# Padding tiles that move the operands of the matmuls within 512 bytes

## The chip, the cores and the metric

One core of one Trainium2 chip runs the kernel. The metric is the device time of one execution in microseconds; 892.1 us is the median of three executions of the kernel before (891.85 to 892.5).

## What is computed

Attention over q, k, v of shape 8 x 8 x 576 x 64 (batch, heads, tokens, head dimension), then a two-layer product over all 4608 tokens. Attention is the sum of two parts: a coarse one over tokens averaged in fours, and a local one in which a token sees three neighbours on either side.

```python
out_d = sm_attn(q_d, k_d, v_d)              # over 144 averaged tokens
out_up = np.repeat(out_d, 4, axis=2)
out_local = ...                             # softmax over |i - j| < 4
x = (out_up + out_local)                    # -> 4608 x 512
h = x @ w_in                                # 512 -> 2048
g = np.maximum(0.01 * h, h)
out = g @ w_out                             # 2048 -> 512
```

## The kernel before

The tokens are cut into ten chunks (0 to 9). Of each chunk the attention part leaves x, transposed, in a tile of the tag x0 or x1 (they alternate): a high half and a low half in fp32r, since every fp32 product is made of three fp32r matmuls (high by high, high by low, low by high). The weights are kept on the chip as high and low halves, too: `wi0` to `wi15` for the first layer, `woh`, `wol` for the second, 128 of the 2048 inner features per index f.

PE then runs two products, chunk by chunk and f by f:

- `up_proj`, L1118: hp += w_in[f] by x. The stationary operand is 128 columns of `wi`, the moving operand is 256 (chunks 0 and 1), 384 (chunks 2 and 3) or 512 columns of x. Twelve matmuls make one bank `hp`.
- `leaky`, L1139 to L1142: ACT writes gh, the high half of the leaky result, and the full result; DVE writes gl, what is left. Both have 512 columns, in three buffers each.
- `down_proj`, L1164: acc += g by w_out[f]. Here the stationary operand is 128 columns of gh or gl, the moving one is 512 columns of `woh` or `wol`: for each 128 tokens the triple (woh, gh), (wol, gh), (woh, gl).

Chunks 8 and 9 go through `up_proj` together at the end, in a scheme with seven products in place of eight (`finale`, L1419). Its stationary operands are `wi` and the sums `sh`, `sl` of weights (made by POOL and ACT in `combine_1`); its moving operands are x of chunk 8, `bh`, `bl`, and four sums T1 to T4 with a high half in a buffer of x1 and low halves in `lo`, `r00`, `r01`, `r10`. These sums come from the last local results: POOL makes them (L944, L1020), DVE reduces them, they go through a buffer in DRAM, DVE adds (L1239), ACT copies the high halves (L1285) into the x1 buffer that chunk 7 has left, and DVE subtracts (L1239 again). Each PE group of three matmuls loads its weights anew, one load to a matmul.

POOL and DVE make the local part: POOL multiplies (L944 for scores, L1020 for values), DVE reduces. All this runs beside the products and feeds the next chunks. The order of the work on each engine is worked out when the kernel is built, by a planner (`Order`) that takes each step's cost and due rank; it knows sizes and engines and no addresses. Each engine runs its instructions in that order.

A tile lies at a byte offset that is the same in all partitions. Pools on the left side are stacked from below (`const`, then `wk`, then those that follow one another above it: `su`, `late`, `last`, `fin1`), each tag of a pool in the order in which it was first asked for; pools on the right side end at the top of the memory. The `wk` pool holds, in this order, olot, x1, x0, three gh, three gl. Nearly all tiles are multiples of 512 bytes, so the byte offsets of the matmuls' operands are these, taken modulo 512 (a slice of a tile keeps it, as slices step by 512 or 2048 bytes):

| tile | pool | offset | modulo 512 |
| --- | --- | --- | --- |
| wi0 to wi8, wol, woh for f = 0 to 8 | const | 896 to 74623 | 384 |
| x1, x0 | wk | 78720, 95104 | 384 |
| gh, gl (three each) | wk | 111488 to 123775 | 384 |
| wi9 to wi15, wol, woh for f = 9 to 15 | late, last | 123776 to 181119 | 384 |
| r11, r10, r00, r01, bh, bl, sr, sh, sl | fin1 | 181120 to 217983 | 384 |
| lo, then sp | fin2, right side | 221152, 225248 | 480, 480 |
| zero operands of the first bf16 matmuls (L342): moving, stationary | x1 | 14592 and 14336 bytes into x1 | 256 bytes apart |
| transposes of the first batch (L606): identity, probabilities | const, su | | 96 to 352 bytes apart |

Of the kernel before, what the change touches and what calls it, by code (L numbers as in the profile page):

```python
# [7 lines left out]
F32 = mybir.dt.float32  # L8
F32R = mybir.dt.float32r
# [80 lines left out]
OMAX = max(c[1] for c in CHUNKS[1:])  # L90
# [142 lines left out]
def attn_moe(ctx: ExitStack, tc, qkt, vm, vr, vmb, vrb, qb, kb, vb, vwb, band, identb, w_in, w_out, ident, edge, out):  # L233
# [3 lines left out]
    wk = ctx.enter_context(tc.tile_pool(name="wk", bufs=1))  # L237
# [11 lines left out]
    def slot(*tags):  # L249
        return (yield ("slot", tags, 0))  # L250

    def sb(s, shape, dtype, pool=None):
        tag = s.tag
        pool = pool or (wk if tag in KEPT else atp if tag in LAND else axp)
        return pool.tile(shape, dtype, name=tag, tag=tag, bufs=bufs[tag])

    def bank(s):
        return ps.tile([128, 512], F32, name=s.tag, tag=s.tag, bufs=bufs[s.tag])

    def op(eng, n, *after, times=1, lock=False):  # L260
        if eng == "PE":
            dur = n
        else:
            a, k = COST[eng]
            dur = times * a + k * n
        return (yield ("op", eng, dur, max((0.0,) + after), 0, after, lock))
# [9 lines left out]
    def wait(name, n=1):  # L276
        return (yield ("wait", name, n))
# [31 lines left out]
    def weight(f, k):  # L309
        f0, _, wis, *ts = max((w for w in wts if w[0] <= f), key=lambda w: w[0])  # L310
        return [w[:, f - f0] for w in ts] if k else [wis[f - f0][:, j] for j in range(2)]
# [5 lines left out]
    weight_tiles(const, 0, FSPLIT)  # L317
    w_out_v = w_out.rearrange("(f p) e -> f p e", p=128)

    stage = [wk.tile([128, bufs["stage"] + 1, HALFS * DM], U16, name="x1", tag="x1", bufs=bufs["x1"])]  # L320
    heads = [stage[0][:, bufs["stage"], i * 2 * DM:(i + 1) * 2 * DM].bitcast(I32) for i in range(bufs["head"])]
    for h in heads:
# [773 lines left out]
    def up_proj():  # L1096
        i = 0
        while i < len(STEPS):
            ch, a, z, f = STEPS[i]
            n = z - a  # L1100
            per = 0.0135 + n / 2400
            m = 2 if (ch, a, f) == (0, 0, 0) else 1
            if f == 0:
                tx = 0.0 if m > 1 else (yield from wait(("x", ch, a), LANDED[ch, a]))
            hps = []
            for k in range(m):
                tw = yield from wait(("w", f + k, 0))
                s_h = yield from slot("hp")
                hps.append((s_h, bank(s_h), weight(f + k, 0), tw))
            xh, xl = (x[:, :, a:z] for x in xt[ch])  # L1110
            for c in range(NC):
                if m > 1:
                    tx = yield from wait(("x", 0, 0, c))
                ws = slice(c * 128, (c + 1) * 128)
                for k, (s_h, hp, w, tw) in enumerate(hps):
                    t = yield from op("PE", 3 * per, tx, tw, s_h.t)
                    for j, (h, x) in enumerate(((1, xh), (1, xl), (0, xh))):
                        nc.tensor.matmul(hp[:, :n], w[h][:, ws], x[:, c], start=c + j == 0, stop=c == NC - 1 and j == 2)  # L1118
                    if c == NC - 1:
                        od.spawn(-205.082, leaky(i + k, n, s_h, hp, t))  # L1120
            if f == NF - 1:
                od.signal(("done", ch), t)
            i += m
# [3 lines left out]
    def leaky(i, n, s_h, hp, t):  # L1127
        pair, second = HALF.get(i, (None, 0))
        if second:
            yield from wait(("pair", pair))  # L1130
            s_g, s_l, gh, gl = pairs.pop(pair)
        else:
            s_g, s_l = (yield from slot("gh")), (yield from slot("gl"))
            gh, gl = sb(s_g, [128, OMAX], F32R), sb(s_l, [128, OMAX], F32R)
            if i in HALF:
                pairs[pair] = s_g, s_l, gh[:, n:], gl[:, n:]
                od.signal(("pair", pair))
        t = yield from op("ACT", 2 * n, t, s_g.t, times=2)
        nc.scalar.activation(out=gh[:, :n], in_=hp[:, :n], func=AF.Prelu, alpha=0.01)  # L1139
        nc.scalar.activation(out=hp[:, :n], in_=hp[:, :n], func=AF.Prelu, alpha=0.01)  # L1140
        t = yield from op("DVE", n, t, s_l.t)
        nc.vector.tensor_tensor(out=gl[:, :n], in0=hp[:, :n], in1=gh[:, :n].bitcast(F32), op=ALU.subtract)  # L1142
        s_h.free(t)
        gs[i] = s_g, s_l, gh, gl
        od.signal(("g", i), t)
# [73 lines left out]
    def unit(pool, tag, shape, dtype):  # L1219
        return fin[pool].tile(shape, dtype, name=tag, tag=tag, bufs=1)  # L1220
# [105 lines left out]
    def follow(key, p, held):  # L1326
# [7 lines left out]
        def first():  # L1334
            t = yield from get("P1")
            s_1, s1 = yield from place()
            t = yield from snap(key, "s1", A(), s1, t, s_1.t)
            t2 = yield from get("P2")
            t = yield from added(B(), s1, ALU.add, t, t2)
            s_1.free(t)  # L1340
            od.spawn(-44.395, leaky(("g", 2 * p), EN, *held["B"], t))

        def rest():
            t = yield from get("P6")
            s_2, u2 = yield from place()
            t2 = yield from snap(key, "u2", A(), u2, t, s_2.t)
            t = yield from get("P7")
            s_3, u3 = yield from place()
            t3 = yield from snap(key, "u3", A(), u3, t, s_3.t)
            t4 = yield from get("P4")  # L1350
            t = yield from added(D(), u3, ALU.add, t3, t4)
            od.spawn(-28.453, leaky(("g", 2 * p + 1), EN, *held["D"], t))
            t4 = yield from get("P3")
            t2 = yield from added(C(), u2, ALU.add, t2, t4)
            s_2.free(t2)
            t3 = yield from added(C(), u3, ALU.subtract, t3, t2)
            s_3.free(t3)
            tg, G = yield from stored(p)
            t = yield from get("P5")
            t = yield from snap(key, "c22", A(), G[:, 1], t, tg)  # L1360
            held["A"][0].free(t)
            t3 = yield from added(C(), G[:, 1], ALU.add, t, t3)
            t = yield from op("ACT", EN, t3)
            nc.scalar.activation(out=G[:, 0], in_=C(), func=AF.Prelu, alpha=0.01)
            held["C"][0].free(t)
            od.signal(("kept", 2 * p), t)
            t = yield from op("ACT", EN, t)
            nc.scalar.activation(out=G[:, 1], in_=G[:, 1], func=AF.Prelu, alpha=0.01)
            od.signal(("kept", 2 * p + 1), t)
# [24 lines left out]
    def finale():  # L1394
        yield from wait(("over", LAST - 2))
        yield from wait("cleared2")
        fin["sp"] = unit(2, "sp", [128, bufs["sp"], EN], F32)
        per = 3 * (0.0135 + EN / 2400)
        for p in range(NP):
            key, held = ("pair", p), {}  # L1400
            ws = [weight(2 * p + i, 0) for i in range(2)]
            raws = dict(A11=[w[:, :256] for w in ws[0]], A12=[w[:, 256:] for w in ws[0]], A22=[w[:, 256:] for w in ws[1]])
            follow(key, p, held)
            for name in ORDER:
                b, a, x = PRODUCTS[name]
                if b not in held:
                    s_b = yield from slot("hp", "pt")
                    held[b] = s_b, bank(s_b)
                tb = held[b][0].t
                if name in BEFORE:  # L1410
                    tb = max(tb, (yield from wait((key, BEFORE[name]))))
                ta = (yield from wait(("sw", 0, p))) if a[0] == "S" else 0.0
                tx = yield from wait(x)
                w = SW[0, p][a] if a[0] == "S" else raws[a]
                for c in range(2):
                    t = yield from op("PE", per, tb, ta, tx)
                    for j, (h, m) in enumerate(((1, 1), (1, 0), (0, 1))):
                        acc = held[b][1][:, :EN]
                        nc.tensor.matmul(acc, w[h][:, c * 128:(c + 1) * 128], T[x][m][:, c],  # L1419
                                         start=c + j == 0 and name not in BEFORE, stop=c == 1 and j == 2, skip_group_check=True)  # L1420
                od.signal((key, name), t)
            od.signal(("paired", p), t)
        od.signal(("done", LAST - 1), t)
# [162 lines left out]
```

## Time and profile before

| | |
| --- | --- |
| median of 3 executions | 892.1 us (891.85 to 892.5) |
| the profiled execution, its time | 893.24 us |
| its span, first to last instruction | 891.5 us |
| matmuls in the trace | 4815, one weight load each |
| mean granted clock of PE | 0.993 of full speed |

The profile shows one execution. PE are the matmuls, PEld the weight loads that run beside them, DVE, ACT and POOL the other engines. A matmul's recorded duration is longer than the distance to the next one's start, as matmuls overlap: 512 columns are recorded with some 390 ns. In the chain that ended last, each piece is counted only up to where the next one begins, so a piece of 24 matmuls divided by 24 is that distance. The granted clock is 1.00 at 2.4 GHz and 0.50 at 1.2 GHz.

### The profile page before, as it was taken

How to read it: one execution, taken by the hardware profiler on the slowest of the kernel's cores; microseconds unless marked ns; L12 is line 12 of the kernel's file. 1: busy time of each engine (PE TensorE's matmuls, PEld its weight loads, DVE VectorE, ACT ScalarE, POOL GpSimd, SP SyncE). 2: the span in 40 equal slices, each digit the busy share in tenths (PEclk: the TensorE clock that was granted, in tenths of full speed). 3: DMA queues.
4: the chain of work that ended last, by engine and by line, in shares of the span. 5: the costliest groups of instructions: out<-in, count | busy, mean ns of one | idle time of the engine just before them, and what ended most of it. 6: DMA issues, size and time to landing. Idle time of an engine off the chain costs nothing.

```text
span 891.5 us, 13603 instructions
## 1 busy us (share of the span) xinstructions
PE 872.8 (98%) x4815; PEld 721.1 (81%) x4815; DVE 639.4 (72%) x952; ACT 461.4 (52%) x1288; POOL 628.9 (71%) x316
## 2 busy tenths in 40 slices
PE   6999999999999999999999999999999999999998
PEld 3687878988899888887888888778878888888886
DVE  5888989888896988898788977887786443323322
ACT  3898866656463744466345635623443244435421
POOL 3434478798999899999998899889976433374000
PEclk9999999999999999999999999999999999999999
DMA  9878764555453563455455535534344000000001
GB/s 336 278 234 293 241 187 133 191 167 186 140 154 111 180 189 113 139 160 171 119 148 174 171 107 160 158 100 116 115 113 137 3 24 24 1 1 1 24 24 48
DMA packets 67684, 119.67 MB, mean 134 GB/s; under 512 B 8608, under 2 KB 34720, under 8 KB 67616
## 3 DMA queue, kind: packets, MB, share of 16 engines
q1 hardware_dynamic: 67616, 118.80, 42.9%
q8 instruction: 38, 0.62, 0.3%
q14 instruction: 30, 0.25, 0.1%
HBM read 106.19 MB, written 12.58 MB: 133 GB/s over the span
## 4 chain that ended last, share of the span: by engine, by line
PE 86%; DVE 6%; DMA 4%; ACT 3%; issue 1%; SPq 0%; POOL 0%; DVEq 0%; POOLq 0%; ACTq 0%
PE acc L1164 35%; PE hp L1118 32%; PE hp L1419 4%; PE pt L1419 4%; DMA qk<-in_qkt_dram 3%; PE hp L1164 2%; PE pt L1164 2%; PE pt L688 1%; DVE xloc L1026 1%; PE pt L707 1%; PE pt L751 1%; DMA stage<-in_w_out_dram 1%; PE pt L710 1%; ACT x L374 1%; DVE gl L1142 0%
## 5 line engine op out<-in xcount | busy, mean ns | idle before, releaser
L1118 PE MATMUL hp<-x,wi 128*128 128x512 f32 (+2 forms) x1632 | 333.7, 356 | 4.1 <-DVE gl L1142 4.1
L1118 PEld LDWEIGHTS hp<-x,wi 128*128 128x128 f32 x1632 | 277.2, 189 | 45.6 <-DVE gl L1142 7.5
L1020 POOL TENSOR_TENSOR prod<-v,sx 128x1344 f32<-128x1344 f32 x84 | 264.3, 3148 | 29.3 <-DVE xloc L1026 16.8
L944 POOL TENSOR_TENSOR prod<-q,k 128x1344 f32<-128x1344 f32 x84 | 261.5, 3114 | 27.4 <-DVE wi L389 8.8
L1164 PE MATMUL acc<-woh,gh 128*128 128x512 f32 x512 | 202.4, 395 | 0.0
L1164 PE MATMUL acc<-wol,gh 128*128 128x512 f32 x512 | 199.9, 390 | 0.0
L1164 PE MATMUL acc<-woh,gl 128*128 128x512 f32 x512 | 199.8, 390 | 0.0
L1139 ACT ACTIVATE gh<-hp 128x512 fp32r<-128x512 f32 (+2 forms) x140 | 73.6, 526 | 143.5 <-PE acc L1164 130.2
L1026 DVE TENSOR_REDUCE xloc<-prod 128x192 f32<-128x1344 f32 x84 | 129.7, 1546 | 14.9 <-POOL prod L1020 14.5
L950 DVE TENSOR_REDUCE s<-prod 128x21 f32<-128x1344 f32 x84 | 129.2, 1538 | 9.7 <-POOL prod L944 9.3
L1142 DVE TENSOR_TENSOR gl<-hp,gh 128x512 fp32r<-128x512 f32 (+2 forms) x140 | 82.8, 594 | 58.5 <-ACT hp L1140 56.2
L1164 PEld LDWEIGHTS acc<-woh,gh 128*128 128x128 f32 x512 | 96.2, 188 | 20.6 <-issue 2.4
L1164 PEld LDWEIGHTS acc<-woh,gl 128*128 128x128 f32 x512 | 96.1, 188 | 20.7 <-DVE gl L1142 0.2
L1164 PEld LDWEIGHTS acc<-wol,gh 128*128 128x128 f32 x512 | 96.2, 188 | 18.0
L1140 ACT ACTIVATE hp<-hp 128x512 f32<-128x512 f32 (+2 forms) x140 | 72.9, 520 | 0.0
L1239 POOL TENSOR_TENSOR sl<-sr,sh 128x1024 fp32r<-128x1024 f32 x8 | 19.2, 2399 | 73.4 <-ACT sh L1243 73.4
L989 ACT COPY sx<-s 32x84 f32<-32x84 f32 x168 | 43.8, 261 | 11.9 <-POOL s L980 9.9
L1323 DVE TENSOR_TENSOR pt<-pt,sp 128x512 f32<-128x512 f32 x12 | 8.4, 699 | 56.4 <-PE pt L1419 31.0
L1050 DVE TENSOR_TENSOR pt<-pt,outd 128x128 f32<-128x128 f32 x126 | 40.1, 322 | 3.1
L445 DVE TENSOR_REDUCE v_d<-vs 128x128 f32<-128x512 f32 (+1 forms) x53 | 35.5, 670 | 5.6 <-DMA vs<-in_vrb_dram 4.4
L1239 DVE TENSOR_TENSOR gl<-wi,gh 128x512 fp32r<-128x512 f32 x14 | 9.7, 692 | 28.3 <-ACT gh L1243 28.3
L742 ACT ACTIVATE pd<-pd,st_d 112x144 f32<-112x144 f32 x72 | 24.5, 405 | 8.9 <-DVE st_d L739 8.8
(228 smaller groups left out, 1127.5 us busy)
## 6 DMA issues: line engine op xcount, KB each, us to landing
k<-in_kb_dram SPq DMA_DIRECT2D x84, 288.0 KB, 3.3
qk<-in_qkt_dram SPq DMA_DIRECT2D x32, 576.0 KB, 4.3
v<-in_vb_dram SPq DMA_DIRECT2D x84, 192.0 KB, 2.6
q<-in_qb_dram SPq DMA_DIRECT2D x84, 96.0 KB, 2.3
vs<-in_vmb_dram SPq DMA_DIRECT2D x28, 256.0 KB, 3.3
out_dram<-olot SPq DMA_DIRECT2D x28, 256.0 KB, 2.1
vs<-in_vrb_dram SPq DMA_DIRECT2D x28, 192.0 KB, 2.7
x<-in_w_out_dram SPq DMA_DIRECT2D x9, 511.8 KB, 6.4
```

The costliest lines, as they stand in the source:

```text
L944: behind(nc.gpsimd.tensor_tensor(out=prv, in0=q[:, :nj].unsqueeze(2).to_broadcast([128, nj, W, D]), in1=view(k, 0, [[D, nj], [D, W], [1, D]]),
L950: nc.vector.tensor_reduce(out=s[:, u, p, :nj], in_=prv, axis=AX.X, op=ALU.add)
L989: nc.scalar.copy(out=both[32 * g:32 * g + 32, :, h], in_=sv[src:src + 32])
L1020: behind(nc.gpsimd.tensor_tensor(out=prv, in0=view(v, 0, [[1, nj], [nv, ROWS], [1, W]]), in1=s[:, p].unsqueeze(2).to_broadcast([128, nj, R ...
L1026: nc.vector.tensor_reduce(out=xl_t[:, :nj, p], in_=prv, axis=AX.X, op=ALU.add)
L1050: nc.vector.tensor_tensor(out=part, in0=part, in1=view(outd[b], 2 * u * SD + o, [[2 * COLS // FAC, ROWS], [sm, cm], [sr, cr]]), op=ALU.add)
L1118: nc.tensor.matmul(hp[:, :n], w[h][:, ws], x[:, c], start=c + j == 0, stop=c == NC - 1 and j == 2)
L1139: nc.scalar.activation(out=gh[:, :n], in_=hp[:, :n], func=AF.Prelu, alpha=0.01)
L1140: nc.scalar.activation(out=hp[:, :n], in_=hp[:, :n], func=AF.Prelu, alpha=0.01)
L1142: nc.vector.tensor_tensor(out=gl[:, :n], in0=hp[:, :n], in1=gh[:, :n].bitcast(F32), op=ALU.subtract)
L1164: nc.tensor.matmul(acc, g[:, ts], w[h], start=f + j == 0, stop=f == NF - 1 and j == 2)
L1419: nc.tensor.matmul(acc, w[h][:, c * 128:(c + 1) * 128], T[x][m][:, c], start=c + j == 0 and name not in BEFORE, stop=c == 1 and j == 2, sk ...
```

## The change

Three tiles are added that no instruction reads or writes: 128 bytes per partition in the pool `wk` ahead of x1, 128 bytes in `wk` between gh and gl (in `leaky`, at the first step alone), and 96 bytes in the pool `fin2` (`unit` asks a pool for a tile).

```diff
     w_out_v = w_out.rearrange("(f p) e -> f p e", p=128)
 
+    wk.tile([128, 32], F32, name="shift0")
     stage = [wk.tile([128, bufs["stage"] + 1, HALFS * DM], U16, name="x1", tag="x1", bufs=bufs["x1"])]
...
             s_g, s_l = (yield from slot("gh")), (yield from slot("gl"))
-            gh, gl = sb(s_g, [128, OMAX], F32R), sb(s_l, [128, OMAX], F32R)
+            gh = sb(s_g, [128, OMAX], F32R)
+            if not i:
+                wk.tile([128, 32], F32, name="shift1")
+            gl = sb(s_l, [128, OMAX], F32R)
             if i in HALF:
...
         yield from wait("cleared2")
+        unit(2, "shift2", [128, 24], F32)
         fin["sp"] = unit(2, "sp", [128, bufs["sp"], EN], F32)
```

## Rows read from the trace of the kernel before

**Rows 1.** The page, part 1: busy time, share of the span, instructions of each engine.
```profile
PE 872.8 (98%) x4815; PEld 721.1 (81%) x4815; DVE 639.4 (72%) x952; ACT 461.4 (52%) x1288; POOL 628.9 (71%) x316
```
**Rows 2.** The page, part 4: the chain that ended last, by engine and by line.
```profile
PE 86%; DVE 6%; DMA 4%; ACT 3%; issue 1%; SPq 0%; POOL 0%; DVEq 0%; POOLq 0%; ACTq 0%
PE acc L1164 35%; PE hp L1118 32%; PE hp L1419 4%; PE pt L1419 4%; DMA qk<-in_qkt_dram 3%; PE hp L1164 2%; PE pt L1164 2%; PE pt L688 1%; DVE xloc L1026 1%; PE pt L707 1%; PE pt L751 1%; DMA stage<-in_w_out_dram 1%; PE pt L710 1%; ACT x L374 1%; DVE gl L1142 0%
```
**Rows 3.** The chain in order of time: start us, us, what; 256, 384, 512 columns.
```profile
171.58 2.87 PE hp L1118 x24
...
225.85 4.18 PE hp L1118 x24
...
427.65 5.44 PE acc L1164 x24
433.09 5.44 PE hp L1118 x24
```
**Rows 4.** PE in order of time near 6 us, and a stretch's busy times and clock.
```profile
5.74 0.81 PE L342 MATMUL acc<-x 128*128 128x512 bf16 x3
...
6.17 0.38 PE L342 MATMUL acc<-x 128*128 128x512 bf16 x1
...
6.00:6.50 0.50, 0.50 (x3) 0.06 (x1) 0.00 (x0) 0.00 (x0) 0.00 (x0) 1.00 0.89 249
```
**Rows 5.** PE in order of time near 21 us, the fp32 transposes.
```profile
20.45 0.27 PE L606 MATMUL pt<-id_sb,v 128*128 128x128 f32 x1
...
20.77 0.49 PE L606 MATMUL pt<-id_sb,v 128*16 128x128 f32 x3
```
**Rows 6.** PE near 209 us, and busy times of PE, PEld, DVE, ACT, POOL, then PEclk.
```profile
208.97 0.84 PE L1118 MATMUL hp<-x,wi 128*128 128x384 f32 x2
...
209.29 0.84 PE L1118 MATMUL hp<-x,wi 128*128 128x384 f32 x2
...
208.60:210.20 1.60, 1.60 (x5) 1.60 (x6) 1.59 (x3) 0.88 (x4) 1.60 (x2) 0.50 0.43 75
```
**Rows 7.** PE and its weight loads in order of time at 686.36 us.
```profile
686.36 0.39 PE L1164 MATMUL acc<-woh,gh 128*128 128x512 f32 x1
...
686.36 0.19 PEld L1164 LDWEIGHTS acc<-wol,gh 128*128 128x128 f32 x1
```
**Rows 8.** PE in order of time from 716.96 us: the matmuls with lo and their neighbours.
```profile
716.96 0.39 PE L1419 MATMUL pt<-x,sh 128*128 128x512 f32 x1
717.18 0.40 PE L1419 MATMUL pt<-lo,sh 128*128 128x512 f32 x1
717.42 0.39 PE L1419 MATMUL pt<-x,sl 128*128 128x512 f32 x1
...
718.34 0.40 PE L1164 MATMUL acc<-woh,gh 128*128 128x512 f32 x1
```
**Rows 9.** L1118's group; then stretches, PE and PEld alone: L1164 whole, L1164, L1419 late.
```profile
L1118 PE MATMUL hp<-x,wi 128*128 128x512 f32 (+2 forms) x1632 | 333.7, 356 | 4.1 <-DVE gl L1142 4.1
...
0.00:891.50 891.50, 416.79 (x1728) 321.00 (x1728) 0.99 0.43 134
...
711.70:891.50 179.80, 101.33 (x432) 81.02 (x432) 1.00 0.05 18
...
711.70:891.50 179.80, 80.01 (x336) 62.40 (x335) 1.00 0.05 18
```
**Rows 10.** Busy times from 111 to 679 us (columns as in rows 6), and a wait of DVE.
```profile
111.00:679.00 568.00, 563.69 (x3077) 473.00 (x3076) 479.48 (x687) 295.95 (x923) 517.79 (x219) 1.00 0.49 147
...
DVE gl L1142 <- ACT hp L1140: 56.2, 46, 4.7
```
**Rows 11.** L1020 on POOL; DVE and ACT in order of time, 699 to 713 us.
```profile
L1020 POOL TENSOR_TENSOR prod<-v,sx x84: 3088/3139/3659, 111.0 to 676.2; 128x1344 f32<-128x1344 f32 x84
...
699.67 2.89 DVE L1239 TENSOR_TENSOR r<-r,r 128x1024 f32<-128x1024 f32 x2
712.80 1.23 DVE L1239 TENSOR_TENSOR lo<-r,x 128x1024 fp32r<-128x1024 f32 x1 [2.16 <-ACT x L1285]
...
711.71 2.00 ACT L1285 CAST x<-r 128x1024 fp32r<-128x1024 f32 x2 [1.80 <-PE hp L1118]
```

## The prediction, made before the changed kernel was run

> **What bounds the kernel now.** I first read the busy shares [rows 1]: PE is at work for 98% of the span, the next engine for 72%. A busy PE can hide waits, so next came the chain that ended last [rows 2]: 86% of it is PE, and its largest lines are the two products (L1118, L1164); DVE, DMA and ACT hold 13% together. So the time is mostly a count of matmuls times the distance between two starts, and what has to be found is what sets that distance. It is not the mean duration of a matmul in the page, since matmuls overlap.
>
> The chain in order of time gives the distance [rows 3]: 24 matmuls of 512 columns take 5.44 us, 226.7 ns each; 24 of 384 columns 4.18 us, 174 ns; 24 of 256 columns 2.87 us, 119.6 ns. A column at the full 2.4 GHz takes 0.417 ns, so the columns alone would take 213.3, 160 and 106.7 ns. The excess is 13 ns in all three cases, about 32 columns for each matmul, whatever its length. It belongs to the pair of matmul and weight load, not to the stream.
>
> Three kinds of rows say when the excess is absent. The bf16 matmuls of 512 columns at the start, at a granted clock of 1.00, follow each other in (0.81 - 0.38)/2 = 0.215 us [rows 4]: 2 ns over their columns. Their operands are two pieces of one tile, 256 bytes apart. The fp32 transposes of 128 columns, which take two columns' time for each, follow in (0.49 - 0.27)/2 = 0.11 us [rows 5], 3 ns over 106.7; their operands never lie at one place modulo 512. And at a granted clock of 0.50 the same fp32r matmul of 384 columns as above, operands at the same place, starts every 0.32 us [rows 6]: 384 columns at 1.2 GHz and nothing more. So the excess needs a 4-byte stream at full clock, and in this kernel every such stream but one has its two operands at one place modulo 512. The weight load of the next matmul starts together with the running matmul (both at 686.36) [rows 7], so the two read streams do run over the same offsets at the same time.
>
> The one exception speaks the other way. The matmuls with `lo` (offset 480, its weights at 384) start 0.24 us before the next matmul, and the six from 716.96 to 718.34 take 230 ns each, not 226.7 [rows 8]. But `lo` is also the only operand that begins at an odd multiple of 32 bytes, so the row mixes two things.
>
> **The change, part by part.** *What moves.* 128 bytes ahead of `x1` put x1, x0 and gh at 0 modulo 512, where they were at 384. Another 128 bytes put gl, and all that is stacked above it (the weights f = 9 to 15, sh, sl, r00 to r11, bh, bl), at 128. 96 bytes in the last pool, if `lo` is laid below them, take it from 480 to 384. Weights f = 0 to 8 stay. So in L1118 the operands come to lie 128 bytes apart for every f; in L1164 gh lies 128 from the weights, gl 256 for f below 9. For f from 9 on gl and the weights are both at 128: still the same place. That is 7 of 16 f's and one of three matmuls, 252 of 1728. In the last products bh, bl, r01 and r10 against sh and sl and half of r00 against its weights stay at one place too, 48 + 32 + 8 = 88. Together 340 of 3696 [rows 9] keep what they have.
>
> *What is added and removed.* No instruction, wait, transfer or step of a queue: three tiles that nobody touches. The order on every engine is worked out from costs that don't hold addresses. DVE, ACT, POOL and DMA work on the shifted tiles is costed at nothing; should one of these rows grow, DVE and ACT (28% and 48% idle, [rows 1]) cover it, and POOL would show it in the middle of the kernel.
>
> *What a matmul gains.* No row has a full-clock fp32r stream with operands 128 or 256 bytes apart at whole lines. Bounds: the bf16 row as the best, 226.7 - 216 = 10.7 ns less; the `lo` row as the worst, 8 ns more for the matmul itself. I take the gain: the bf16 row is the nearest in length, clock and distance (256), and `lo` differs in alignment, which the change mends. Over 3696 - 340 = 3356 matmuls it is 36 us of PE time at most.
>
> *What of it reaches the end.* After 711.7 us PE runs the last products and the last L1164 with nothing else to wait for: 432 + 336 = 768 matmuls [rows 9]. Of these 72 of L1164 (gl with f from 9 on: 56 of the last two chunks, 16 of the one before) and the 88 above stay at one place, so 608 x 10.7 = 6.5 us come off. Ahead of 711.7 PE would gain up to 29 us, but it would meet the other chain: POOL works 518 of 568 us between 111 and 679 [rows 10], its last local product starts at 676.2, and DVE closes the sums that the last products need at 702.56 (699.67 + 2.89) [rows 11]. They are then copied by ACT (711.71) into a buffer that PE frees at the end of L1118, and split by DVE (712.80) [rows 11]. With PE early, the copy can start at 702.6, not 711.71: 9.1 us. Beyond that the POOL chain itself has to come earlier. It idles 50 us in its stretch, partly behind a DVE that waits for PE (DVE's gl waited 56.2 us for ACT, which waits for PE [rows 10]). I take 5 us, an estimate between 0 and 10. A wait of PE of many microseconds there may cost a spell at half clock as at 208.6 [rows 6], where 5 matmuls lost 0.15 us each: 1 us. Mending `lo`: 16 matmuls, 8 times some 0.03 us, 0.2 us, inside the rounding.
>
> Sum: 6.5 + 9.1 + 5 - 1 = 20 us. The profiled execution took 893.2 us for a span of 891.5, 1.1 us over the median of 892.1, and its times are taken as they are: 892.1 - 20 = **872 us**. With no help from POOL and two thirds of the gain in each matmul it is 882; with POOL 10 us earlier and a little more of PE's 29 us it is 862. That is this case's own range.
>
> **The rivals.** *Nothing changes.* The excess is the price of a weight load beside a 4-byte stream, wherever they lie. For it: 13 ns at three lengths, and no excess at half clock with operands at one place, as if it were a matter of rate alone; the bf16 and transpose rows also read at half the rate, so they don't single out the place. Against it: `lo` shows that an address can change the distance at all. Time: 892 less 0.2 for `lo`, 892.
>
> The Trainium skill, "SBUF — State Buffer", section "Who interferes with whom", sides with it: it gives PE two read ports, one for the moving operand and one for LDWEIGHTS, independent, and says that PE and ACT never wait on anyone. By that rule the change is worth nothing; that the fp32r rows take 13 ns over their columns and the bf16 rows 2 is something that the rule does not tell. The same page's 16-byte cachelines make 32 lines of a 512-byte row of weights, the number of columns in the excess, which fits either case.
>
> *Slower: the steady beat is lost.* At one common offset the matmuls run in a steady 226.7; one `lo` in three matmuls lifts six of them to 230 [rows 8]. After the change the three matmuls of L1164 have distances of 128, 128 and 256 or 0, so the place changes from one to the next all the time. It decides when a triple of L1164 takes over 0.68 us. At 3.3 ns for each of 3696 it is 12.2 us, 904; on L1164 alone (1728) 5.7 us, 898; at the 8 ns of `lo` itself on all, 30 us, 922. PE's time is the span's here, so all of it lands. For it: it is the only fp32r row with another distance. Against it: the alignment of `lo`.
>
> **How the numbers follow.** Gain 0.45, nothing 0.28, slower 0.27. Rows for the gain are of other types, the row for the loss is of another alignment, and the even excess suits nothing, so no case has half. The likeliest gives 872. The range of 862 to 904 holds nearly all of the first case, the second and about half of the third, 8 in 10. Under 0.2% (1.8 us) a measurement of this kernel can't be told from no change; the cases lie on either side of that bound, so the chances are faster 0.45, same 0.28, slower 0.27.
>
> **What would show it.** Right: L1118 and L1164 pieces of 24 matmuls take 5.2 us in place of 5.44, those of 384 columns 3.9 to 4.0, except gl at f from 9 on; the six with `lo` fall in line; PE waits between 680 and 705; ACT's copy into x starts near 702, and more of the chain is POOL and DVE. Nothing: 5.44 stays and only the `lo` pieces shrink. Slower: 5.44 grows to 5.5 to 5.65 and the chain stays with PE. The step most likely wrong is the price of a matmul, after it the 5 us of POOL.

## The result, and the profile after

| | before | after |
| --- | --- | --- |
| median of 4 executions, taken beside each other on one chip | 891.98 us (890.98 to 892.5) | 904.68 us (902.15 to 905.65) |
| ratio | | 1.0139, 95% interval 1.0115 to 1.0164 |
| the profiled execution, its time and span | 893.24, 891.5 us | 903.79, 902.0 us |

The kernel became 12.7 us slower; the forecast was 20 us faster. Nothing that moves or copies data changed. In the page's part 1 of the kernel after (busy time, share of the span, instructions), beside [rows 1], one number moves: PE has 11.1 us more (the trace lacks six of its matmul records), the rest stays within 1.3 us.

```profile
PE 883.9 (98%) x4809; PEld 719.9 (80%) x4815; DVE 639.6 (71%) x952; ACT 460.9 (51%) x1288; POOL 627.6 (70%) x316
```

Part 4 of the same page, the chain that ended last, has still more of PE: 90%, where it was 86% [rows 2], and the two products, now L1168 and L1119, have 38% and 33%, where they had 35% and 32%. These shares can't price the change, since the chain also took another way: in its first 120 us the two products now hold 43%, and held 26%. The pieces of the chain can.

```profile
PE 90%; DMA 3%; DVE 3%; ACT 2%; issue 1%; SPq 0%; POOL 0%; DVEq 0%; POOLq 0%
PE acc L1168 38%; PE hp L1119 33%; PE hp L1424 4%; PE pt L1424 4%; PE hp L1168 2%; PE pt L1168 2%; PE pt L689 1%; DVE x L1243 1%; DMA su_vs<-in_vm_dram 1%; PE pt L708 1%; PE pt L752 1%; DMA qk<-in_qkt_dram 1%; DMA su_vs<-in_vwb_dram 1%; DMA stage<-in_w_out_dram 1%; DVE xloc L1027 1%
```

The chain in order of time (start, us, what) shows it piece by piece. With 256 columns a piece takes as before, 2.88 us for 2.87. With 384 it takes 4.23 for 4.18. With 512 it takes 5.59 for 5.44 [rows 3], which is 232.9 ns for a matmul in place of 226.7.

```profile
188.26 2.88 PE hp L1119 x24
...
213.72 4.23 PE hp L1119 x24
...
422.75 5.59 PE hp L1119 x24
428.34 5.59 PE acc L1168 x24
433.93 5.59 PE hp L1119 x24
```

Below, "the step" is the time between the starts of two fp32r matmuls that follow each other without a wait, averaged over all such pairs of a group in the trace. For 512 columns it went from 227.6 to 232.6 in L1119 and from 227.9 to 232.7 in L1168. So 864 x 5.0 = 4.3 us came on L1119, 1728 x 4.8 = 8.3 on L1168, about 384 x 1.2 = 0.5 on the 384 columns and 336 x 2.6 = 0.9 on the last products: 14 us of steps, where the median shows 12.7 and PE's busy time 11.1. Part of the difference may be the clock: its mean was 0.993 in the profiled execution before and is 0.998 in this one.

The other engines only waited longer. The busy times of 111 to 679 us (columns as in rows 6) show PE full at a granted clock of 1.00, as before, and POOL with 510 us of work for 518 [rows 10], so the clock isn't the cause. DVE waits 69.5 us for ACT, and so for PE, where it waited 56.2. POOL's last local product starts at 682.8, 6.6 us later than in [rows 11], and ACT's copy into x at 719.18, 7.5 us later; the end follows it by 182.8 us, which were 179.8 (432 x 4.8 + 336 x 2.6 ns are 2.9 us of these 3).

```profile
111.00:679.00 568.00, 565.36 (x3047) 468.22 (x3046) 472.09 (x678) 292.05 (x913) 509.93 (x217) 1.00 0.49 145
...
DVE gl L1146 <- ACT hp L1144: 69.5, 63, 5.3
...
719.18 2.00 ACT L1289 CAST x<-r 128x1024 fp32r<-128x1024 f32 x2 [1.88 <-PE hp L1119]
```

The one step that went as foretold is `lo`. PE in order of time (start, recorded duration, what) has its matmul 0.22 us ahead of the next one, where [rows 8] has 0.24. `lo` is now 256 bytes from `sh`. Over its sixteen matmuls the mean step went from 233.2 to 227.9 ns.

```profile
724.54 0.39 PE L1424 MATMUL pt<-x,sh 128*128 128x512 f32 x1
724.77 0.39 PE L1424 MATMUL pt<-lo,sh 128*128 128x512 f32 x1
724.99 0.39 PE L1424 MATMUL pt<-x,sl 128*128 128x512 f32 x1
...
725.91 0.39 PE L1168 MATMUL acc<-woh,gh 128*128 128x512 f32 x1
```

### The profile page after: what moved, and what is told of

Read it like the earlier page. It is cut to its first block, busy times and chain, and to the rows that moved or that the text cites. A ratio compares the mean times of both kernels' runs of the same rounds, so it can differ in the third digit from the quotient of the medians.

```text
span 902.0 us, 13597 instructions
## 1 busy us (share of the span) xinstructions
PE 883.9 (98%) x4809; PEld 719.9 (80%) x4815; DVE 639.6 (71%) x952; ACT 460.9 (51%) x1288; POOL 627.6 (70%) x316
## 4 chain that ended last, share of the span: by engine, by line
PE 90%; DMA 3%; DVE 3%; ACT 2%; issue 1%; SPq 0%; POOL 0%; DVEq 0%; POOLq 0%
PE acc L1168 38%; PE hp L1119 33%; PE hp L1424 4%; PE pt L1424 4%; PE hp L1168 2%; PE pt L1168 2%; PE pt L689 1%; DVE x L1243 1%; DMA su_vs<-in_vm_dram 1%; PE pt L708 1%; PE pt L752 1%; DMA qk<-in_qkt_dram 1%; DMA su_vs<-in_vwb_dram 1%; DMA stage<-in_w_out_dram 1%; DVE xloc L1027 1%
## 5 line engine op out<-in xcount | busy, mean ns | idle before, releaser
L1119 PE MATMUL hp<-x,wi 128*128 128x512 f32 (+2 forms) x1632 | 338.4, 359 | 3.9 <-DVE gl L1146 3.9
L1119 PEld LDWEIGHTS hp<-x,wi 128*128 128x128 f32 x1632 | 277.7, 189 | 49.6 <-DVE gl L1146 7.4
L1168 PE MATMUL acc<-woh,gh 128*128 128x512 f32 x512 | 204.5, 399 | 0.0
L1168 PE MATMUL acc<-woh,gl 128*128 128x512 f32 x512 | 202.4, 395 | 0.0
L1168 PE MATMUL acc<-wol,gh 128*128 128x512 f32 x512 | 201.8, 394 | 0.0
L1146 DVE TENSOR_TENSOR gl<-hp,gh 128x512 fp32r<-128x512 f32 (+2 forms) x140 | 83.1, 595 | 71.9 <-ACT hp L1144 69.5
L1168 PEld LDWEIGHTS acc<-woh,gl 128*128 128x128 f32 x512 | 96.1, 188 | 22.9 <-DVE gl L1146 0.2
L1168 PEld LDWEIGHTS acc<-woh,gh 128*128 128x128 f32 x512 | 96.2, 188 | 22.4 <-issue 2.4
L1168 PEld LDWEIGHTS acc<-wol,gh 128*128 128x128 f32 x512 | 96.4, 188 | 20.3
```

The lines of the kernel that those rows point to most:

```text
L1168: nc.tensor.matmul(acc, g[:, ts], w[h], start=f + j == 0, stop=f == NF - 1 and j == 2)
```

## The experiments

Four theories were open: that the *place* counts (384 modulo 512 is good, 0 is bad); that the *distance* from the stationary to the moving operand counts; that the *alternation* of distances within a triple breaks the beat; and that the *alignment* of an operand to less than 64 or 128 bytes costs more than the rest. Each kernel is the kernel before with padding tiles that nobody touches, or with x started some columns later in its tile. Distances are those of the moving operand minus the stationary one, in bytes. Each run has its own ratio to the kernel before, run beside it.

**1. All at another place.** 128 bytes below the first weight put every operand of the two products at 0 modulo 512, with all distances at 0.

```diff
+    const.tile([128, 32], F32, name="pad_c")
     weight_tiles(const, 0, FSPLIT)
```

> All operands of the matmuls moved by 128 bytes together, from 384 to 0 modulo 512; their distance stays 0. Distance theory (the step between two matmuls depends on how far the moving and the stationary operand lie apart): 24 matmuls of 512 columns still take 5.44 us, time 892 within 1 us. Place theory (what counts is where an operand begins in its 512 bytes, 384 being a good place and 0 and 128 bad ones): 24 matmuls take 5.58 to 5.60 us as in the changed kernel, time 900 to 907.

891.24 us, ratio 0.9992 (0.9976 to 1.0008). The chain in order of time has the old pieces:

```profile
419.98 5.44 PE hp L1119 x24
425.42 5.44 PE acc L1165 x24
```

So 0 is no worse a place than 384 as long as all operands share it. What is left is what lies between two operands.

**2. One constant distance.** 128 bytes ahead of gh move gh, gl and the weights from f = 9 on. Now L1167 has 128 for f below 9 and 0 from 9 on; L1118 has 0 below 9 and 128 from 9 on. Within a triple nothing alternates.

```diff
+            if not i:
+                wk.tile([128, 32], F32, name="pad_g")
+            gh = sb(s_g, [128, OMAX], F32R)
```

> 128 bytes ahead of gh alone: gh and gl lie together, 128 bytes from the weights of f below 9 and 0 from those of f from 9 on; x lies 0 from the weights of f below 9 and 128 from the others. The distance is the same for all three matmuls of a triple. Distance theory: L1167 pieces of 24 take 5.6 us for f below 9 and 5.44 from 9 on, L1118 the other way round, so a little over half of the matmuls lose 6 ns: time 898 to 901. Alternation theory (the steady beat is lost because the distance changes from one matmul of a triple to the next): all pieces of 24 at 5.44, time 892. Place theory (x stays at 384, gh and gl go to 0): L1118 keeps 5.44 for f below 9, all of L1167 slow, 901 to 904.

900.17 us, 1.0094 (1.0067 to 1.0121). In the chain in order of time L1118 takes 5.45 us at f below 9, 5.59 from 9 on, and L1167, at f above 9 at that moment, 5.46:

```profile
355.44 5.45 PE hp L1118 x24
...
421.42 5.59 PE hp L1118 x24
427.01 5.46 PE acc L1167 x24
```

The same line of the same kernel takes either value, by its distance alone. A constant 128 is enough for the loss, so alternation isn't needed. The steps agree with the total: 972 of L1167 x 4.6 ns + 420 of L1118 with 512 columns x 5.0 ns + some 1.5 us for the rest (0.7 of it the last products) = 8.0 us, measured 8.4 by the ratio (6.0 to 10.8).

**3 to 6. Other distances.** Two pads set the distances: the first moves x, gh and gl, both together move the weights from f = 9 on. The edit is the same in all four, with these bytes for A and B: 64 and 64; 32 and 32; 160 and 192; 224 and 96.

```diff
+    wk.tile([128, A // 4], F32, name="pad_x")
     stage = [wk.tile([128, bufs["stage"] + 1, HALFS * DM], U16, name="x1", tag="x1", bufs=bufs["x1"])]
...
             gl = sb(s_l, [128, OMAX], F32R)
+            if not i:
+                wk.tile([128, B // 4], F32, name="pad_e")
```

> 64 bytes ahead of x1 and 64 behind gl: every pair of the two products lies 64 bytes apart (plus or minus), constant within a product. Distance theory, with a loss at any distance but 0: 24 matmuls at 5.5 to 5.65 us, 900 to 910. If only the distance modulo 64 counted, or if 128 were an unlucky distance among many good ones: 5.44, 892. A gain to 5.3 or less (distance clears a conflict, as I had predicted for 128) would give 880 to 885.

> 32 bytes ahead of x1 and 32 behind gl: every pair lies 32 bytes apart, and the tiles begin at odd multiples of 32 bytes, as lo does in the kernel before. Distance theory with a loss that grows with distance: between 892 and 903, 24 matmuls at 5.45 to 5.55 us. Distance theory with a loss at any distance but 0: 900 to 910. Alignment theory (lo was slow because it began at an odd multiple of 32): 24 matmuls at 5.6 us or more, over 905.

> 160 bytes ahead of x1, 192 behind gl: in L1119 the moving operand lies 160 above the weights (modulo 512) for f below 9 and 192 below them from 9 on, in L1168 the other way round. If only the distance 0 keeps the short step of 226.7 ns: 24 matmuls of 512 columns at 5.5 to 5.65 us everywhere, 900 to 907. If some other distance gives a step of 220 ns (5.28 us for 24) or less, as bf16's 216 once let me hope, this is one of the three kernels that must show it.

> 224 bytes ahead of x1, 96 behind gl: distances 224 above and 96 below in L1119, 224 below and 96 above in L1168. Only distance 0 good: 5.5 to 5.65 us for 24 matmuls, 900 to 907. 96 is the distance of lo in the kernel before, without its wait for other neighbours: by lo's own step 5.64 us for 24.

In this order: 901.63 us, 1.0102 (1.0075 to 1.0129); 905.1, 1.014 (1.0116 to 1.0163); 906.42, 1.0165 (1.0141 to 1.0188); 905.0, 1.0151 (1.0128 to 1.0174). From the chain in order of time, the kernel with 64:

```profile
422.64 5.60 PE hp L1119 x24
```

the kernel with 32:

```profile
421.47 5.60 PE hp L1119 x24
427.08 5.60 PE acc L1168 x24
```

and the one with 224 and 96:

```profile
422.93 5.62 PE hp L1119 x24
428.55 5.61 PE acc L1168 x24
```

No distance was found that shortens the step of 512 columns. Run 4 by itself, at 905.1 us and 5.60, would also fit the alignment theory. But odd multiples of 32 (233.1 to 234.0 ns) cost about what 128 costs (232.4 to 233.0), an aligned distance, so alignment isn't needed for the loss. Only +64 has a value between: 229.4, and 231.3 at -192, the same modulo 256, against 233.2 at -64.

**7. 256 against 32 in one kernel.** 256 ahead of x1, 32 behind gl: for f below 9 the distances are 256 up and down, above 9 they are 32.

```diff
+    wk.tile([128, 64], F32, name="pad_x")
...
+                wk.tile([128, 8], F32, name="pad_e")
```

> 256 bytes ahead of x1, 32 behind gl: distances 256 for f below 9 in both products, 32 for the others. Only distance 0 good: 5.5 to 5.65 us for 24 matmuls, 900 to 907; at 32 as in the kernel with 32 everywhere, 5.59. If 256, the distance of the bf16 operands, clears a conflict: 5.2 to 5.3 us for f below 9 and 880 to 885.

897.8 us, 1.0074 (1.0051 to 1.0096). The chain in order of time passes from L1168 at f below 9 to L1119 above it:

```profile
582.26 5.45 PE acc L1168 x24
587.70 5.59 PE hp L1119 x24
```

256 bytes are as good as none.

**8. A version that might beat both.** In the kernel with 64 the 256-column matmuls at a distance of -64 took 113.8 ns on average, not 119.3. So x of chunk 1 was started at column 240, which is 64 bytes below modulo 256, and `lo` got its 96 bytes.

```diff
-        both = whole[:, :, :, :CHUNKS[i][1]]
+        c0 = 240 if i == 1 else 0
+        both = whole[:, :, :, c0:c0 + CHUNKS[i][1]]
...
+        unit(2, "pad_lo", [128, 24], F32)
```

> The kernel before with lo alone moved to 384 (96 bytes behind it in its pool) and x of chunk 1, 256 columns wide, at columns 240 to 495 of its tile, 64 bytes below the weights. Distance theory: the 16 matmuls with lo and their neighbours at 226.7 ns (1.36 us for six in place of 1.39), 24 matmuls of chunk 1 at 2.72 us in place of 2.87 as the kernel with 64 showed, together 0.25 and 1.1 us of PE time: 890.8 to 892.2, of which the 1.1 us can be lost to waits for x between 150 and 200 us. Place or alignment theory: no change in chunk 1.

890.23 us against 891.26, 0.9988 (0.9973 to 1.0002). In the chain in order of time the pieces of chunk 1 shrink from 2.87 us:

```profile
169.36 2.75 PE hp L1119 x24
...
181.17 2.73 PE hp L1119 x24
```

The pieces show the effect. The total can't be told from no change: 192 matmuls x 5 ns are 1 us.

**9. Alternation alone.** 256 bytes between gh and gl let the distances of a triple alternate between 0 and 256.

```diff
             gh = sb(s_g, [128, OMAX], F32R)
+            if not i:
+                wk.tile([128, 64], F32, name="pad_l")
             gl = sb(s_l, [128, OMAX], F32R)
```

> 256 bytes ahead of gl alone: within each triple of L1167 the distance now changes, 0 and 256, and is 0 or 256 everywhere else. Distance theory with a period of 256 bytes (what the kernel with 256 ahead of x1 suggests): 24 matmuls at 5.44 us in both products, 891 to 892. Alternation theory (my rival: a changing distance breaks the steady beat): L1167 at 5.5 us or more for 24, 897 to 904, L1118 at 5.44.

891.89 us against 892.04, 0.9988 (0.9973 to 1.0004). Every piece in the chain in order of time is at the old value:

```profile
580.78 5.44 PE acc L1167 x24
586.22 5.44 PE hp L1118 x24
```

Changing from one place to another costs nothing as long as the distances agree modulo 256.

**10 and 11. Under 32 bytes.** x was put some columns further into a tile that is 8 columns longer, which gives distances of -16, +16 and -48 (with 224 bytes ahead of x1), and +8 and +48 (with 192 bytes ahead of gh, which keeps L1168 at 0).

```diff
-        whole = sb(s_x, [128, 2, NC, 512], F32R)
+        o = (4, 4)[i % 2]
+        whole = sb(s_x, [128, 2 * NC * 512 + 8], F32R)[:, o:o + 2 * NC * 512].rearrange("p (h c n) -> p h c n", h=2, c=NC)
```

In the second `o = (4, 2)[i % 2]`.

> Finer distances in L1120: 16 below the weights for x in x1 and 16 above for x in x0 at f below 9, 48 and 16 below from f = 9 on; gh and gl 32 below at f below 9, 0 from 9 on. Distance theory with 0 the best: 24 matmuls of 512 columns in L1120 at 5.48 to 5.6 us, 897 to 905. If the step has its least value at some distance of a few bytes (the weight load runs some 3 ns behind the matmul it starts with), one of the groups in L1120 shows 5.28 us for 24.

> In L1119 x lies 8 bytes above the weights (x1) or 48 (x0), modulo 256; L1168 keeps 0, modulo 256. Distance theory: L1168 at 5.44 us for 24, L1119 at 5.46 to 5.6, 893 to 897. A better distance than 0 at 8 or 48: L1119 pieces under 5.4.

903.57 us, 1.0116 (1.0082 to 1.0151), and 896.77, 1.0054 (1.0036 to 1.0072). In the chain in order of time of the first, only L1166 from f = 9 on, where gh and gl have a distance of 0, has the old piece. The first line is x0 at -16, the last x1 at -16:

```profile
423.33 5.60 PE hp L1120 x24
428.93 5.44 PE acc L1166 x24
...
457.23 5.68 PE hp L1120 x24
```

and in that of the second L1168 has it, while L1119, with x1 at +8, has not:

```profile
426.40 5.47 PE acc L1168 x24
...
442.91 5.60 PE hp L1119 x24
```

Eight or sixteen bytes are enough to lose about as much as 128 do, so there is no gentle slope from 0. The distance modulo 256 doesn't tell all: at -16, x0 with f from 9 on takes 232.6 ns, and x1 with f below 9, at +240 modulo 512, takes 235.7, the worst of all.

**12. x alone.** 128 ahead of x1 and 128 ahead of gh: x lies 128 from the weights for every f, gh and gl 0 or 256 from them.

```diff
+    wk.tile([128, 32], F32, name="pad_x")
...
+            if not i:
+                wk.tile([128, 32], F32, name="pad_g")
```

> 128 bytes ahead of x1 and 128 ahead of gh: x lies 128 from the weights for every f, gh and gl 0 or 256. The half of the change that L1119 carries. Distance theory with period 256: L1119 at 5.59 us for 24 and L1168 at 5.44; 816 matmuls of 512 columns lose 5 ns, 384 of 384 columns 1.2, the sums in L1423 some 3 ns: 896 to 898.

896.71 us, 1.0048 (1.0033 to 1.0063), 4.7 us more by the medians and 4.3 by the ratio. One product in the chain in order of time is slow, the other isn't:

```profile
420.87 5.59 PE hp L1119 x24
426.46 5.45 PE acc L1168 x24
```

That is the share of x in the change: by the steps 4.4 us on L1119's 864 matmuls of 512 columns (the expectation counts 816), 0.5 on those of 384 and 0.9 on the last products, whose x is moved here too. The other 8 of the 12.7 us are L1168's.

**All distances together.** The step of 512 columns once it has settled (the mean of those with at least nine matmuls of the same product ahead of them and no wait between), by distance modulo 256:

| distance | step, ns | from kernel |
| --- | --- | --- |
| 0 (0 or 256) | 226.7 to 228.0 | before, 1, 2, 7, 9 to 12 |
| +8, +16 | 232.8, 231.8 | 11, 10 |
| +32, +48 | 233.1 to 233.3, 233.3 | 4, 6, 7; 11 |
| +64 (+64; -192) | 229.4; 231.3 | 3; 5 |
| +96, 128 | 233.1, 232.4 to 233.0 | 5, 6; after, 2, 12 |
| -96 (-96; +160) | 234.0; 233.9 | 6; 5 |
| -64 (-64; +192) | 233.2; 233.2 | 3; 5 |
| -48, -32 | 232.9, 233.2 to 233.4 | 10; 4, 6, 7, 10 |
| -16 (-16; +240) | 232.6; 235.7 | 10 |

Distances that differ by 256 agree within some 0.3 ns at 128, 96, 32, 8, -32, -64 and -96 and within 1 at 0, but not at +64 and -16, where they differ by 2 and 3 ns.

## Why the prediction was wrong

**The step that failed** is "What a matmul gains": "I take the gain: the bf16 row is the nearest in length, clock and distance (256), and `lo` differs in alignment, which the change mends." It priced a matmul at -10.7 ns, and the runs showed +5.0 on 512 columns, +1.2 on 384 and none on 256. Two things were wrong in it. The bf16 row's distance of 256 is in fact the same as 0 (runs 7 and 9), so the row said nothing of 128. And the `lo` row, put aside for its alignment, was the only fp32r row at a distance that isn't a multiple of 256. Its six matmuls at 230 ns were the first sight of the loss: runs 4 and 6 gave odd multiples of 32 no price of their own. The row nearest in the type of its data was the right one.

**What bounds the kernel** held: PE's step sets the time, and nearly all of the loss landed, 12.7 of 14 us. **The layout** held too as arithmetic. But "together 340 of 3696 keep what they have" did not. In the trace of after gl's matmuls in L1168, a third of that product, lie at 0 or 256 for every f, and their settled step is 234.2 ns against 232.9 for gh's at 128. A matmul's own distance doesn't decide alone: the load that runs beside it is that of the next matmul [rows 7], and beside gl's it is the next gh, 128 bytes from what is streamed. Run 2 shows that this second pair counts. At f below 9 its L1118 lies at 0 from its own weights, and beside the last matmul before L1167 the load is that of gh, 128 away: this matmul takes 232.5 ns (mean of 19 settled ones), where it took 226.4 in before. Nor is a good second pair enough: (wol, gh) in after, at 128 from gh and with gl at 0 or 256 loaded beside it, takes 232.9. And good pairs among bad ones may not settle: the 48 matmuls of bh and bl, all at 0, went from 228.7 to 231.1, while those of `lo` gained.

**What reaches the end** (6.5 us of tail, 9.1 of the copy, 5 of POOL) never came into play: with PE late, the copy came 7.5 us later and POOL's last product 6.6 us later. The sum of 20 us fell with its first factor. The 1 us for a spell at half clock wasn't tested either; ahead of the one at 208.6 the longest wait of PE was 1.22 us, not many microseconds. **Mending `lo`** held [rows 8], and stayed inside the rounding as foretold.

**The rival "nothing changes"** was wrong with its reason, that the excess is "a matter of rate alone": at one rate and one clock the step changes by 3% with the distance. It was right in one thing: nothing that was tried takes the 13 ns over the columns away with 512 columns, so no run shows them to be the price of lying at one place. The Trainium skill, "SBUF — State Buffer", section "Who interferes with whom", has PE's two read ports independent. If that were all, the step could not depend on the distance between what the two read. It does: 5.45 against 5.59 us a piece in run 2, for one line in one kernel. The measurement decides. That the two reads get in each other's way is a reading of it; the runs show the dependence on the distance, not the mechanism.

**The rival "the steady beat is lost"** had the time (904), the engine and the mark by which to know it (L1168 over 0.68 us a triple, which is 0.70). Its reason was half right. The steady beat is lost, but a change of distance within a triple isn't what it takes: run 9 changes it between 0 and 256 at no cost, and L1119, with one constant distance, loses as much. What a change between unlike distances costs by itself no run tells apart. Its 3.3 ns, a mean over `lo` and its neighbours, was 5 on 512 columns, and it was put on all 3696 matmuls, where those of 256 columns lose nothing and those of 384 lose 1.2: two errors that nearly cancel, so that its time was luck in part. Its upper price, 8 ns for `lo` itself, was too high: the sixteen take 233.2 ns, 6.5 more. The range ended at its 904, which the measurement passed by 0.7.

**What stays open:** by what mechanism the distance acts, why 0 and 256 are alike while +64 and -192 or -16 and +240 are not, and why +64 differs from -64.

## What to carry to other kernels

In an fp32r kernel with wide matmuls, look first whether moving and stationary operands lie at distances that are multiples of 256 bytes, and keep them there: any tile that isn't a multiple of 256 bytes shifts all that is stacked above it, and in this kernel 128 bytes cost 5 ns of 227 in each matmul of 512 columns. Count the operand that is loaded beside a matmul, too, not only its own. Read the step from the chain (a piece divided by its count), by product and by length; PE's busy share stayed at 98%, and L1168's mean duration moved from 390 to 394 ns for (wol, gh), where the step moved by 2%. When no row shows the new state, take the bound from the row with the same type of data first, even if something else about it differs.

## What the runs showed that was not expected

- *A good step must settle.* After a change of product the first nine matmuls of before take 227 to 231 ns on average, and from the tenth on they hold 226.7 in L1164 and 227.1 in L1118. At 128 they never settle to one value: in L1119 of after they alternate between 229 and 238, in L1168 they repeat 232, 233 and 235.
- *The best distance depends on the length.* With 256 columns 0 is not the best: the mean step is 119.3 ns there, 119.2 at 128, 122.4 at +8, 117.4 at +32 (run 4), and 113.8 and 114.6 at -64 (runs 3 and 8), 4 to 5% less than at 0. With 384 columns the settled step is 173.3 at 0, 175.5 at 128 and 180 at -16. A piece of 256 columns at -64, from the chain in order of time of run 3:

```profile
184.26 2.72 PE hp L1119 x24
```

- *The step at 0 is exact.* Settled, 226.7, 173.3 and 120 ns are the time of 544, 416 and 288 columns at 2.4 GHz: the columns and 32 more. At the granted clock of 0.50 [rows 6] the 32 are not there: 384 columns take 0.32 us.
